# Four sums of weight blocks per chunk, on GpSimd in place of VectorE, in a gated attention and ReGLU kernel

## The chip, the cores and the metric

The kernel runs on one core of a Trainium2 chip. The metric is the device time of one execution in microseconds; the time before is the median of 3 runs. In the profile the engines are called PE (TensorE matmuls), PEld (TensorE weight loads, which overlap PE), DVE (VectorE), ACT (ScalarE), POOL (GpSimd) and SP (SyncE, which issues the DMAs here). L621 is line 621 of the kernel.

## What is computed

Two branches on the same x (2048 tokens, width 576) and a gate between them. Branch a is a linear attention with 32 heads of 18; branch b is a gated feed-forward layer with 4608 hidden columns. All is float32.

```
g = sigmoid(sum(x * gate_w))                      # one gate per token
q, k, v = x @ wqkv, by heads
phi(u) = [softmax(u @ w_phi), softmax(-u @ w_phi)]
a = (phi(q) (phi(k)^T v) / (phi(q) phi(k)^T 1)) @ wo
gate, up = x @ W_gate, x @ W_up                   # 576 x 4608 each
h = max(gate, 0) * up
b = h @ W_down                                    # 4608 x 576
out = g * a + (1 - g) * b
```

The change lies in branch b, in the weights of gate and up.

## The kernel before

**Split operands.** Matmuls run in the format fp32r. To keep float32 accuracy each operand is split: ACT copies it to fp32r (the high part), and DVE subtracts that from the original (the low part). A product is then three matmuls: high by high, high by low, low by high.

**Stages.** The first stage makes queries, keys, values and the attention; its result goes to a DRAM tensor `att`. The second is branch b. It goes through 72 units: two halves of the tokens (1024 each, in two blocks of 512) by 36 chunks of 128 hidden columns (L596). Between the halves the operands made of x are built again (`x_operands`, L560), and the finished tiles of the first half are written out (`finish`, L727).

**Seven products in place of eight.** Gate and up of a chunk, for two blocks of tokens, split along the 576 inputs into two halves of 288, are eight products of blocks. The kernel makes them with seven, of sums and differences of blocks. So a unit needs the four raw blocks of weights and four combinations of them:
- `load_w` (L598) brings the four blocks of a unit into one tile `wr` of 128 partitions by 4 x 384 elements, one of two buffers, by one DMA from SP.
- `split_blocks` (L610) makes `wb`, the split of three raw blocks: an ACT copy (L604) and two DVE subtractions (L607, L608). It serves the products 1, 2 and 4.
- `split_sums` (L617) first overwrites `wr` with the four combinations (L621 to L624, each 128 x 384 elements, each needing the one before), then makes `ws`, the split of all four: the same lines L604, L607, L608. It serves the products 5, 6, 7 and 3.

Both are traced for unit u + 1 while unit u is computed (L795, L801). The tiles `wb` and `ws` have two buffers each.

**One unit on PE.** Each product is seven matmuls at L720, in the order 1, 5, 6, 7, 2, 3, 4. Products 1, 6, 7 and 4 accumulate in one PSUM tile `cx` (two buffers); 5 and 3 in `ca`; 2 in `cy`. Between them the partial results are taken out: ACT copies cx to g1 (L789), ca to u2 (L794), cx to g2 (L800); DVE adds cx to u2 (L805), cy to g1 (L810), ca to g2 (L815). At the end DVE multiplies gate and up (L822), and `split` makes hh and hl of the result (L123, L124).

**The down projection.** `down` (L744) runs for a pair of units, spread as steps between the products of the next pair. Each step is a group of matmuls at L763 into a PSUM tile `pd` (two buffers), which DVE adds to an accumulator in SBUF (L770), or into one of two tiles `pm` that stay in PSUM. `split_down` (L703) prepares its weights `wd`.

**The order of the work.** The program is traced in the order of the code, and a planner then sets the order of each engine's queue from the priorities of the trace and its own costs. On the engine each queue is worked off in that fixed order, an instruction waiting for the semaphores of its inputs and of the buffers it overwrites. Where `in_order` is used (L49: parts of `x_operands` in the first stage's end) the order of the trace is kept on DVE, ACT and SP. POOL serves the first stage only: it scales half of each tile of softmax terms (L182), and sets some constants (L259, L403).

Of the kernel before, what the change touches and what calls it, by code (L numbers as in the profile page):

```python
# [62 lines left out]
def gated_mix_kernel(  # L63
# [25 lines left out]
    nc = tc.nc  # L89
    PSUM = bass.MemoryType.PSUM  # L90
    SUB, ADD, MULT = ALU.subtract, ALU.add, ALU.mult
    tt = nc.vector.tensor_tensor
# [510 lines left out]
    def split_w(o, a, after=None):  # L603
        i = nc.scalar.activation(o[:, :, 0:3], a, AF.Copy)  # L604
        if after:
            tc.add_manual_dep(i.ins, after.ins.name, NO_SYNC, reason="after")
        tt(out=o[:, :, 3:5], in0=a[:, :, 0:2], in1=o[:, :, 0:2].bitcast(F32), op=SUB)  # L607
        tt(out=o[64:96, :, 2], in0=a[64:96, :, 2], in1=o[64:96, :, 2].bitcast(F32), op=SUB)  # L608
# [8 lines left out]
    def split_sums(u):  # L617

        if u < len(units):
            a = RAW.pop(u)  # L620
            tt(out=a[:, 2], in0=a[:, 2], in1=a[:, 3], op=ADD)  # L621
            tt(out=a[:, 3], in0=a[:, 0], in1=a[:, 3], op=SUB)
            tt(out=a[:, 0], in0=a[:, 2], in1=a[:, 0], op=SUB)
            tt(out=a[:, 1], in0=a[:, 1], in1=a[:, 0], op=SUB)  # L624
            o = wop.tile([P, 4, 5, P], F32R, name="ws")
            split_w(o, a)
            WO[u].update({5: (o, 2), 6: (o, 0), 7: (o, 3), 3: (o, 1)})
# [12 lines left out]
    for n, tb in enumerate(order):  # L640
# [23 lines left out]
        if not more:  # L664
            split_blocks(0)
            split_sums(0)
# [115 lines left out]
    for u, (hf, c) in enumerate(units):  # L782
# [16 lines left out]
        g2 = tp.tile([P, TB], F32, name="g2", tag="tp")  # L799
        nc.scalar.activation(g2, cx, AF.Copy)  # L800
        split_sums(u + 1)  # L801
        step()
        product(cx, u, 7, False)
# [117 lines left out]
```

## Time and profile before

| | us |
|---|---|
| median of 3 runs | 1706.8 |
| lowest and highest | 1704.52 and 1708.77 |
| the profiled execution | 1707.41 |
| its span on the core | 1705.6 |

The mean granted clock of PE in the profiled execution is 0.98 of full speed. The groups of instructions which the change touches or which stand next to it, each 72 times in the program (busy us in total, then the mean ns of one):

| line, engine | what | busy us, mean ns |
|---|---|---|
| L622, L623, L624 DVE | sums in wr, 128 x 384 | 40.1, 557 each |
| L604 ACT | copy to ws, 128 x 1536 | 107.3, 1490 |
| L607 DVE | low part of ws, 128 x 1024 | 88.2, 1225 |
| L608 DVE | low part of ws, 32 x 512 | 49.2, 683 |
| L607 DVE | low part of wb, 128 x 768 | 69.0, 958 |
| L608 DVE | low part of wb, 32 x 384 | 39.6, 550 |

A row of the views used below is read so: in the rows of groups, line, engine, operation, output <- inputs, sizes, the count, then busy time and mean, then the idle time of the engine ahead of the group and what ended it. In rows in order of time, the start in us from the beginning of the span and the duration come first; "x7" is seven instructions merged into one row, and the bracket gives the idle time just before and what ended it. In the chain of waits, each piece is on the chain that ended last, followed back from the last instruction.

### The profile page before, as it was taken

How to read it: one execution, taken by the hardware profiler on the slowest of the kernel's cores; microseconds unless marked ns; L12 is line 12 of the kernel's file. 1: busy time of each engine (PE TensorE's matmuls, PEld its weight loads, DVE VectorE, ACT ScalarE, POOL GpSimd, SP SyncE). 2: the span in 40 equal slices, each digit the busy share in tenths (PEclk: the TensorE clock that was granted, in tenths of full speed). 3: DMA queues.
4: the chain of work that ended last, by engine and by line, in shares of the span. 5: the costliest groups of instructions: out<-in, count | busy, mean ns of one | idle time of the engine just before them, and what ended most of it. 6: DMA issues, size and time to landing. Idle time of an engine off the chain costs nothing.

```text
span 1705.6 us, 19899 instructions
## 1 busy us (share of the span) xinstructions
PE 1648.6 (97%) x7834; PEld 1379.0 (81%) x7834; DVE 1291.1 (76%) x1966; ACT 624.0 (37%) x895; POOL 46.0 (3%) x53
## 2 busy tenths in 40 slices
PE   9999997988999999999999998999999999999996
PEld 8899995666888888888888886788888888888885
DVE  5877675666778777777778779977777777777776
ACT  4233335554533333333323334433333332333330
POOL 0121210000000000000000000000000000000000
PEclk9899997889999999999999999999999999999998
DMA  5211113535221211122122212421111222121203
GB/s 182 69 37 58 44 44 96 170 127 169 83 70 65 70 51 60 61 65 70 51 70 66 70 51 70 149 83 62 63 61 52 70 65 70 51 70 60 63 18 105
DMA packets 42329, 128.48 MB, mean 75 GB/s; under 512 B 4906, under 2 KB 5546, under 8 KB 42236
## 3 DMA queue, kind: packets, MB, share of 16 engines
q1 hardware_dynamic: 42236, 127.22, 23.1%
q8 instruction: 61, 1.00, 0.2%
q14 instruction: 32, 0.26, 0.0%
HBM read 108.50 MB, written 16.74 MB: 73 GB/s over the span
## 4 chain that ended last, share of the span: by engine, by line
PE 86%; DVE 5%; DMA 4%; ACT 2%; issue 1%; SPq 1%; DVEq 0%; ACTq 0%
PE cx L720 26%; PE pd L763 19%; PE ca L720 13%; PE cy L720 6%; PE pm L763 5%; PE pq L150 4%; PE pk L150 3%; PE pv L150 3%; PE kv L319 2%; PE pwo L150 2%; PE ptr L283 1%; DMA ga<-att 1%; PE po L150 1%; DMA xr<-xs 1%; DMA wdr<-wd 1%
## 5 line engine op out<-in xcount | busy, mean ns | idle before, releaser
L763 PE MATMUL pd<-hh,wd 128*128 128x512 f32 x1008 | 357.5, 390 | 2.2 <-DVE ac L770 2.2
L720 PE MATMUL cx<-xo,ws 128*128 128x512 f32 x1008 | 253.2, 390 | 5.3 <-DVE ws L608 2.2
L720 PE MATMUL cx<-xo,wb 128*128 128x512 f32 x1008 | 252.5, 390 | 2.8 <-DVE o L556 1.4
L720 PE MATMUL ca<-xo,ws 128*128 128x512 f32 x1008 | 253.4, 390 | 0.8 <-DVE ws L608 0.6
L720 PEld LDWEIGHTS cx<-xo,ws 128*128 128x128 f32 x1008 | 188.8, 188 | 46.6 <-ACT g L789 2.7
L763 PE MATMUL pd<-hl,wd 128*128 128x512 f32 x576 | 224.6, 390 | 0.0
L720 PEld LDWEIGHTS cx<-xo,wb 128*128 128x128 f32 x1008 | 188.9, 188 | 43.8 <-DVE o L556 1.9
L763 PEld LDWEIGHTS pd<-hh,wd 128*128 128x128 f32 x1008 | 189.4, 188 | 43.1 <-DVE ac L770 3.5
L720 PEld LDWEIGHTS ca<-xo,ws 128*128 128x128 f32 x1008 | 189.2, 188 | 42.2 <-ACT wd L708 1.0
L770 DVE TENSOR_TENSOR ac<-pd,ac 128x512 f32<-128x512 f32 x272 | 187.5, 690 | 33.1 <-PE pd L763 33.1
L123 ACT ACTIVATE hh<-g 128x512 fp32r<-128x512 f32 x144 | 83.0, 621 | 294.3 <-DVE g L822 294.3
L708 ACT ACTIVATE wd<-wdr 128x576 fp32r<-128x576 f32 x72 | 48.8, 679 | 262.2 <-PE pd L763 256.0
L604 ACT ACTIVATE ws<-wr 128x1536 fp32r<-128x1536 f32 x72 | 107.3, 1490 | 59.5 <-DVE wr L624 59.5
L720 PE MATMUL cy<-xo,wb 128*128 128x512 f32 x504 | 126.6, 389 | 0.0
L763 PEld LDWEIGHTS pd<-hl,wd 128*128 128x128 f32 x576 | 108.4, 188 | 22.4
L607 DVE TENSOR_TENSOR ws<-wr,ws 128x1024 fp32r<-128x1024 f32 x72 | 88.2, 1225 | 44.1 <-ACT ws L604 43.9
L607 DVE TENSOR_TENSOR wb<-wr,wb 128x768 fp32r<-128x768 f32 x72 | 69.0, 958 | 55.1 <-ACT wb L604 53.5
L720 PEld LDWEIGHTS cy<-xo,wb 128*128 128x128 f32 x504 | 94.6, 188 | 19.6
L763 PE MATMUL pm<-hh,wd 128*128 128x512 f32 x288 | 101.0, 389 | 0.0
L800 ACT ACTIVATE g<-cx 128x512 f32<-128x512 f32 x72 | 43.1, 598 | 153.4 <-PE cx L720 147.4
L822 DVE SCALAR_TENSOR_TENSOR g<-g,cx 128x512 f32<-128x512 f32 x72 | 49.5, 687 | 60.2 <-PE cx L720 60.1
L815 DVE TENSOR_TENSOR g<-ca,g 128x512 f32<-128x512 f32 x72 | 49.8, 691 | 58.4 <-PE ca L720 58.3
(180 smaller groups left out, 2555.2 us busy)
## 6 DMA issues: line engine op xcount, KB each, us to landing
wr<-wgu SPq DMA_DIRECT2D x72, 768.0 KB
wdr<-wd SPq DMA_DIRECT2D x72, 288.0 KB
eT<-et SPq DMA_DIRECT2D x12, 594.0 KB
er<-eT SPq DMA_DIRECT2D x12, 594.0 KB
xr<-xs SPq DMA_DIRECT2D x8, 768.0 KB
att<-o SPq DMA_DIRECT2D x16, 256.0 KB
ga<-att SPq DMA_DIRECT2D x16, 256.0 KB
outT<-o SPq DMA_DIRECT2D x16, 256.0 KB
```

Of the source, the lines that this page charges most:

```text
L123: nc.scalar.activation(hi, src, AF.Copy)
L150: nc.tensor.matmul(ps, w, m, start=i == 0, stop=i == len(pairs) - 1)
L319: nc.tensor.matmul(kv[j // 2][:vn + 1, j % 2, :gn], v[:, j * GS:j * GS + vn + 1], flat(e)[:, c0:c0 + gn], start=False, stop=t == NT - 1, s ...
L604: i = nc.scalar.activation(o[:, :, 0:3], a, AF.Copy)
L607: tt(out=o[:, :, 3:5], in0=a[:, :, 0:2], in1=o[:, :, 0:2].bitcast(F32), op=SUB)
L708: nc.scalar.activation(o[:, :D], w, AF.Copy)
L720: nc.tensor.matmul(ps, w, v, start=first and m == 0, stop=m == len(pairs) - 1, skip_group_check=True)
L763: nc.tensor.matmul(ps, w, v, start=i == 0 and (g == 0 or not perm), stop=i == len(pairs) - 1 and (g == NGR - 1 or not perm))
L770: tt(out=ACC[m, t], in0=ps, in1=ACC[m, t], op=ADD)
L800: nc.scalar.activation(g2, cx, AF.Copy)
L815: tt(out=g2, in0=ca, in1=g2, op=ADD)
L822: nc.vector.scalar_tensor_tensor(out=g, in0=g, scalar=0.0, in1=up, op0=ALU.max, op1=MULT)
```

## The change

The four combinations are issued on GpSimd with the same operands, in the same place of the trace; nothing else is altered.

```diff
         if u < len(units):
             a = RAW.pop(u)
-            tt(out=a[:, 2], in0=a[:, 2], in1=a[:, 3], op=ADD)
-            tt(out=a[:, 3], in0=a[:, 0], in1=a[:, 3], op=SUB)
-            tt(out=a[:, 0], in0=a[:, 2], in1=a[:, 0], op=SUB)
-            tt(out=a[:, 1], in0=a[:, 1], in1=a[:, 0], op=SUB)
+            pt = nc.gpsimd.tensor_tensor
+            pt(out=a[:, 2], in0=a[:, 2], in1=a[:, 3], op=ADD)
+            pt(out=a[:, 3], in0=a[:, 0], in1=a[:, 3], op=SUB)
+            pt(out=a[:, 0], in0=a[:, 2], in1=a[:, 0], op=SUB)
+            pt(out=a[:, 1], in0=a[:, 1], in1=a[:, 0], op=SUB)
             o = wop.tile([P, 4, 5, P], F32R, name="ws")
             split_w(o, a)
             WO[u].update({5: (o, 2), 6: (o, 0), 7: (o, 3), 3: (o, 1)})
```

`tt` is `nc.vector.tensor_tensor`. The subtractions of `split_w` stay on DVE.

## The prediction

> **What bounds the kernel now.** I read the page first: the span and the shares.
>
> ```profile
> span 1705.6 us, 19899 instructions
> ...
> PE 1648.6 (97%) x7834; PEld 1379.0 (81%) x7834; DVE 1291.1 (76%) x1966; ACT 624.0 (37%) x895; POOL 46.0 (3%) x53
> ```
>
> PE is the bound on average and DVE is second. An average says little about a change inside one stage, so I cut the span into stretches (busy us of PE, PEld, DVE, ACT, POOL in each, with counts).
>
> ```profile
> core 0: us, PE busy (x) PEld busy (x) DVE busy (x) ACT busy (x) POOL busy (x), PEclk, DMA share, GB/s
> 380.00:420.00 40.00, 35.68 (x146) 27.83 (x145) 26.96 (x34) 17.36 (x23) 0.00 (x0) 0.96 0.51 166
> 600.00:1018.00 418.00, 418.00 (x1846) 346.24 (x1845) 325.78 (x503) 141.22 (x192) 0.00 (x0) 1.00 0.19 63
> 1018.00:1108.00 90.00, 82.64 (x341) 63.29 (x340) 84.74 (x124) 41.05 (x50) 0.00 (x0) 0.98 0.33 102
> 1036.00:1090.00 54.00, 47.40 (x190) 35.83 (x191) 52.57 (x80) 19.30 (x23) 0.00 (x0) 0.97 0.43 137
> 1108.00:1640.00 532.00, 532.00 (x2348) 440.53 (x2347) 415.05 (x641) 181.93 (x246) 0.00 (x0) 1.00 0.19 63
> ```
>
> There are three places to judge. In the **steady stage** (600 to 1018 and 1108 to 1640) PE is busy for every microsecond, 418.00 of 418.00 and 532.00 of 532.00, so a lighter DVE can gain nothing there; it can only lose. At the **turn** between the two halves (1018 to 1108) PE loses 90.00 - 82.64 = 7.36 us, and within it DVE is busy 52.57 of 54.00 us: here DVE is the bound. At the **start** (380 to 420) PE loses 4.3 us. POOL is empty in all of them.
>
> **What goes.** Four DVE instructions of each of 72 chunks; one of the four groups, with two groups used further down:
>
> ```profile
> L621 DVE TENSOR_TENSOR wr<-wr 128x384 f32<-128x384 f32 x72 | 40.2, 558 | 2.3
> ...
> L604 ACT ACTIVATE wb<-wr 128x1152 fp32r<-128x1152 f32 x72 | 83.3, 1157 | 0.1
> ...
> L259 POOL MEMSET vt<- 128x6 f32 x16 | 1.7, 108 | 40.3 <-ACT gs L258 21.9 <-ACT vt L255 18.4
> ```
>
> That is 4 x 40.2 = 161 us of DVE, and 1291 falls to about 1130.
>
> **What comes.** The same four on POOL. Before, POOL has no sum of 384 elements; its nearest rows are the multiplications of 576 at L182 (minimum/median/maximum ns), and two of them in order of time (start, duration):
>
> ```profile
> L182 POOL TENSOR_TENSOR e<-e,sm x16: 1181/1668/1692, 41.2 to 246.0; 128x576 f32<-128x576 f32 x16
> L182 DVE TENSOR_TENSOR e<-e,sm x16: 758/760/1492, 41.5 to 246.3; 128x576 f32<-128x576 f32 x16
> L182 POOL TENSOR_TENSOR e<-e,r x16: 1163/1168/1176, 67.0 to 264.9; 128x576 f32<-128x576 f32 x16
> ...
> 245.73 0.69 DVE L170 TENSOR_REDUCE mn<-pq 128x32 f32<-128x576 f32 x1
> ...
> 245.98 1.19 POOL L182 TENSOR_TENSOR e<-e,sm 128x576 f32<-128x576 f32 x1 [5.74 <-DVE sm L244]
> 246.34 1.44 DVE L182 TENSOR_TENSOR e<-e,sm 128x576 f32<-128x576 f32 x1
> ```
>
> The queries' product (e<-e,r) takes 1168 ns undisturbed. If all of that scales with the elements, 384 cost 779 ns; if none does, 1168. The memset of 6 elements took 108 ns, so I take 0.11 as the fixed part: 0.11 + (1.17 - 0.11) x 384/576 = 0.82 us. Each sum reads what the one before wrote, so they run one after the other; I allow 0.05 between them and ahead of the first. The chain is 4 x 0.82 + 4 x 0.05 = 3.5 us, with ends at 4 x 0.78 + 0.1 = 3.2 and 4 x 1.17 + 0.2 = 4.9.
>
> The same rows show that the two engines get in each other's way. At 245.98 POOL was first and took 1.19, and DVE's own product, started at 246.34, took 1.44 in place of 0.76. Usually it is POOL that waits: 1668 in place of 1168. The Trainium skill (SBUF — State Buffer, section Who interferes with whom) says that a DVE instruction with two SBUF inputs and a GpSimd instruction that reads SBUF exclude each other for a whole instruction; these rows agree, with 0.5 us lost on POOL or 0.7 on DVE.
>
> **The steady stage.** One chunk there, DVE with the instructions of the others that matter (start, duration):
>
> ```profile
> 813.58 0.56 DVE L621 TENSOR_TENSOR wr<-wr 128x384 f32<-128x384 f32 x1
> ...
> 815.36 0.56 DVE L624 TENSOR_TENSOR wr<-wr 128x384 f32<-128x384 f32 x1
> ...
> 815.95 1.49 ACT L604 ACTIVATE ws<-wr 128x1536 fp32r<-128x1536 f32 x1 [0.54 <-DVE wr L624]
> ...
> 816.18 0.69 DVE L770 TENSOR_TENSOR ac<-pd,ac 128x512 f32<-128x512 f32 x1 [0.26 <-PE pd L763]
> ...
> 817.48 1.23 DVE L607 TENSOR_TENSOR ws<-wr,ws 128x1024 fp32r<-128x1024 f32 x1 [0.61 <-ACT ws L604]
> ...
> 818.72 0.68 DVE L608 TENSOR_TENSOR ws<-wr,ws 32x512 fp32r<-32x512 f32 x1
> ...
> 819.43 0.69 DVE L805 TENSOR_TENSOR u<-cx,u 128x512 f32<-128x512 f32 x1
> ...
> 820.71 0.69 DVE L770 TENSOR_TENSOR ac<-pd,ac 128x512 f32<-128x512 f32 x1
> ...
> 822.30 0.69 DVE L815 TENSOR_TENSOR g<-ca,g 128x512 f32<-128x512 f32 x1 [0.90 <-PE ca L720]
> ...
> 823.46 1.75 PE L720 MATMUL cx<-xo,wb 128*128 128x512 f32 x7
> ...
> 825.04 0.39 PE L763 MATMUL pd<-hh,wd 128*128 128x512 f32 x1
> ...
> 825.70 0.69 ACT L708 ACTIVATE wd<-wdr 128x576 fp32r<-128x576 f32 x1 [8.25 <-PE pd L763]
> ...
> 827.53 0.84 PE L720 MATMUL ca<-xo,ws 128*128 128x512 f32 x3
> ```
>
> The four sums run from 813.58 to 815.92: 2.34 us. On POOL they take 3.5, so the copy to ws, and the DVE instructions behind it, come 1.1 us later (0.9 to 2.6 by the ends). That is the added wait: DVE stands at L607 until POOL and then ACT are done, with L608, L805, L810, L770 and L815 queued behind. Who waits for them:
> - ws is ready at 819.40 and first read at 827.53: cover 8.1 us.
> - L805 is done at 820.12, and PE adds to the same cx at 823.46: cover 3.3 us. This is the shortest.
> - The L770 of 820.71 is done at 821.40 and its bank, one of two, is filled again at 825.04: cover 3.6 us.
> - L815 already waits 0.90 for PE, so a lag of that size ends there.
> - ACT's next instruction behind the copy is L708, after 8.25 idle. POOL has nothing else to do.
> - The next load of wr waits for L608, but a chunk's buffer is read again only later: the 72 copies to wb that read these loads stood idle 0.1 us in all.
>
> So 1.1 us, and even 2.6, lies under 3.3 us: I cost the steady stage at **0**. If the cover went, each microsecond beyond 3.3 would be paid in some 70 chunks. Beside POOL's chain DVE has only L770 to do, which has one input in PSUM; the reduction of a PSUM tile (L170, 245.73) beside the POOL product of 245.98 left that at 1.19, so I expect no clash.
>
> **The turn.** The chain of waits here runs through DVE, sums included, up to the split of ws, and PE waits for that:
>
> ```profile
> 1028.97 0.56 DVE wr L621
> ...
> 1031.20 0.47 DVE wr L622
> ...
> 1035.20 0.56 DVE wr L623
> ...
> 1036.36 0.47 DVE wr L624
> ...
> PE cx L720 <- DVE ws L608: 2.2, 1, 2.2
> ```
>
> The sums' pieces are 0.56 + 0.47 + 0.56 + 0.47 = 2.06 us, about as much as PE's wait for L608 (2.2). They go. What is late next is the rest of DVE's queue, the operands of the second half, and behind them the transfers of the finishing tiles, so I count nothing for the other chunks of the turn. Given back: DVE's work here is mostly SBUF with SBUF, so a POOL sum and a DVE instruction can exclude each other. By the median row POOL waits and DVE loses 0; by the row of 246.34 DVE could lose a whole sum, 0.82. I take 0.15 for each of the four, nearer to the median: 0.6. The turn: -2.06 + 0.6 = **-1.5**, with ends at -7.4 (all that PE loses) and +4 x 0.82 - 2.06 = +1.2 for one chunk.
>
> **The start.**
>
> ```profile
> 380.49 0.56 DVE L621 TENSOR_TENSOR wr<-wr 128x384 f32<-128x384 f32 x1
> ...
> 383.02 0.55 DVE L624 TENSOR_TENSOR wr<-wr 128x384 f32<-128x384 f32 x1
> ...
> 387.34 0.69 DVE L124 TENSOR_TENSOR rdl<-rd,rdh 128x512 fp32r<-128x512 f32 x1 [0.29 <-DMA R<-og]
> ```
>
> Here other work stood between the sums: 380.49 to 383.57, 3.08 us. On POOL 3.5, so 0.4 late, of which 0.29 is hidden by the wait for a DMA at 387.34: **+0.1** (up to 4.9 - 3.08 - 0.29 = +1.5).
>
> **Sum.** 0 - 1.5 + 0.1 = -1.4 us. The profiled execution took 1707.41 us (1705.6 of it span); 1707.4 - 1.4 = 1706.0. Its own lead over the median 1706.8 is 0.6. About 0.3% (5.1 us) is what a measurement of this kernel can tell from no change, and -1.4 lies well inside.
>
> **Rivals.**
> - *DVE's relief empties the turn.* DVE is busy 52.57 of 54.00 us there and loses the sums of three chunks, 3 x 2.2 = 6.7 us. If all of it reaches PE, 1707.4 - 6.7 = 1700.7. For it: the DVE share. Against: transfers end waits in that stretch too, and the sums do not lie in the chain of every chunk. Chance 0.12.
> - *The two engines exclude each other at the turn.* Three chunks with four sums, each holding up DVE by 0.82, cost 9.8 us, less the 2.06 won, plus 1.5 at the start: +9, at 1716. This is the mechanism of the page on SBUF. For it: the row of 1.44. Against: the medians, by which POOL is the one that waits. Chance 0.12.
> - *POOL's chain overruns the cover in the steady stage; slower.* Place: DVE's queue behind L607, ended by PE waiting at the product into cx for L805. Price: if every sum took the 1.67 of the disturbed rows, 4 x 1.67 + 0.2 = 6.9, which is 4.5 late, 1.2 over the cover, in 70 chunks 84 us: 1791. It decides from (2.34 + 3.3 - 0.2) / 4 = 1.36 us a sum. For it: such times occur. Against: only L770 runs beside the sums. Chance 0.06.
> - *The change does not do what it says:* the instructions are named for POOL outright, so only the planned order of the other queues is free. A new order may fill DVE's gap with splits of SBUF data; one or two clashes of 0.5 us still fit under 3.3. It is in the forecast's width.
>
> **How the numbers follow.** Forecast (within 0.3%): 0.70. Faster by over 0.3%: 0.12, the first rival. Slower by over 0.3%: 0.12 + 0.06 = 0.18. The range goes from the first rival's 1700 to just short of the second's 1716: 1700 to 1715; it leaves out the 0.06 and some of the other edges.
>
> **What would show it.** POOL busy at 46 + 288 x 0.82 = 282 us, DVE at about 1130, both long stretches of PE still full, and the copy to ws waiting for POOL about 1.1 us more each. Wrong would be: a sum over 1.36 us in the steady stage; PE waiting for L805 or L770 in every chunk; a turn in which PE loses much more or less than 6 us.

## The result, and the profile after

| | before | after |
|---|---|---|
| median, us | 1705.55 (6 runs, the 3 of the table ahead of the prediction among them) | 1724.82 (6 runs) |
| lowest and highest, us | 1703.57 and 1708.77 | 1718.18 and 1727.52 |
| the profiled execution, us | 1707.41 | 1718.18 |

The ratio after to before (of the means) is 1.0107, with a 95% interval of 1.0087 to 1.0126: some 18 us slower. The profiled execution of after is its fastest; it lies 10.8 us above that of before, and the typical one another 6.6 above it. Part of this is luck ahead of the change: the four matmuls at L504, shortly before the first moved sum (376.2 us), start at 372.3 us in the trace of before and at 367.8 in that of after. Counted from there, the two executions differ by 15.3 us.

The page of after first: its span, the shares of the engines, and three groups (line, engine, operation, tiles, count | busy us, mean ns of one | idle us of the engine just before, and what ended it).

```profile
span 1716.4 us, 19978 instructions
...
PE 1647.0 (96%) x7834; PEld 1376.5 (80%) x7834; DVE 1128.0 (66%) x1678; ACT 622.2 (36%) x895; POOL 344.6 (20%) x341
...
L622 POOL TENSOR_TENSOR wr<-wr 128x384 f32<-128x384 f32 x72 | 74.3, 1032 | 1081.1 <-issue 836.8
...
L607 DVE TENSOR_TENSOR ws<-wr,ws 128x1024 fp32r<-128x1024 f32 x72 | 88.2, 1225 | 196.5 <-ACT ws L604 196.5
L604 ACT ACTIVATE ws<-wr 128x1536 fp32r<-128x1536 f32 x72 | 107.1, 1488 | 211.1 <-POOL wr L625 211.1
```

DVE has lost 1291.1 - 1128.0 = 163 us of work, as it should, and PE has as much work as before, yet the span has grown by 10.8 us. The two big idle times, 196.5 us of DVE at L607 and 211.1 us of ACT at the copy to ws, look like the culprit. Most of that idle time costs nothing, as the same stretches before and after show (us, then busy us and count of PE, PEld, DVE, ACT and POOL, PEclk, DMA share, GB/s). Before:

```profile
420.00:470.00 50.00, 48.12 (x211) 39.11 (x210) 38.33 (x61) 24.44 (x34) 0.00 (x0) 1.00 0.27 86
1015.00:1125.00 110.00, 102.64 (x429) 79.73 (x428) 100.56 (x149) 50.11 (x64) 0.00 (x0) 0.98 0.32 100
```

After:

```profile
380.00:420.00 40.00, 34.17 (x137) 26.67 (x136) 23.98 (x29) 19.00 (x25) 0.80 (x1) 0.91 0.53 175
420.00:470.00 50.00, 46.16 (x198) 36.13 (x197) 28.92 (x41) 20.69 (x30) 16.35 (x16) 1.00 0.23 74
600.00:1018.00 418.00, 418.00 (x1846) 346.16 (x1845) 266.37 (x408) 142.03 (x192) 97.30 (x96) 1.00 0.19 62
1015.00:1125.00 110.00, 95.19 (x390) 73.69 (x389) 91.13 (x120) 43.53 (x54) 25.08 (x20) 0.97 0.31 97
1125.00:1660.00 535.00, 535.00 (x2362) 443.04 (x2362) 342.37 (x523) 183.68 (x250) 124.14 (x123) 1.00 0.19 61
```

The steady stage is full of PE as before: 418.00 of 418.00, 535.00 of 535.00, with the same 1846 and 2362 matmuls. PE's idle time grew at the turn, from 7.36 to 14.81 us (+7.45), and at the start, from 4.32 to 5.83 in 380 to 420 (+1.5) and from 1.88 to 3.84 in 420 to 470 (+2.0). That makes 10.9 us of idle time. It equals the difference of the spans by chance: it leaves out the 4.5 us by which after was ahead at L504, and what PE loses while it is busy at a reduced clock (PEclk 0.91 against 0.96 in 380 to 420).

So the stages are timed by PE's own work as well, from the L504 group to the first matmul into `cy` (product 2) of units 6, 34, 42 and 71, counted from 0. The start, up to unit 6, takes 148.6 us before and 154.8 after (+6.2). From unit 6 to 34 it is 488.69 in both, and from 42 to 71 it is 506.15 in both. The turn, from unit 34 to 42, takes 152.7 before and 161.6 after (+8.9).

What PE waits for at the turn, 1015 to 1125, by the view of the waits of after (us in all, times, longest), and DVE's wait there for ACT's copy, which was 0.4 us before:

```profile
PE cx L721 <- DVE u L806: 6.0, 2, 3.2
PE pd L764 <- DVE ac L771: 3.2, 3, 1.4
PE ca L721 <- DVE ws L608: 2.7, 1, 2.7
...
DVE ws L607 <- ACT ws L604: 8.6, 4, 2.4
```

PE waits for DVE still, although DVE has less to do. The rows of the first unit of the turn in order of time, DVE and POOL of after, show why:

```profile
1028.24 1.01 POOL L622 TENSOR_TENSOR wr<-wr 128x384 f32<-128x384 f32 x1 [16.48 <-ACT xo L569]
...
1028.74 1.59 DVE L570 TENSOR_TENSOR xo<-xr,xo 128x1024 fp32r<-128x1024 f32 x1
1029.33 1.88 POOL L623 TENSOR_TENSOR wr<-wr 128x384 f32<-128x384 f32 x1
1030.35 1.40 DVE L571 TENSOR_TENSOR xo<-xr,xo 32x512 fp32r<-32x512 f32 x1
1031.28 1.34 POOL L624 TENSOR_TENSOR wr<-wr 128x384 f32<-128x384 f32 x1
1031.78 2.46 DVE L583 TENSOR_TENSOR xr<-xr,xr 128x1536 f32<-128x1536 f32 x1
1032.71 2.41 POOL L625 TENSOR_TENSOR wr<-wr 128x384 f32<-128x384 f32 x1
1034.16 2.57 DVE L580 TENSOR_TENSOR xr<-xr,xr 128x1536 f32<-128x1536 f32 x1
...
1039.83 1.22 DVE L570 TENSOR_TENSOR xo<-xr,xo 128x1024 fp32r<-128x1024 f32 x1
1041.06 0.68 DVE L571 TENSOR_TENSOR xo<-xr,xo 32x512 fp32r<-32x512 f32 x1
```

L570 and L571 take 1.22 and 0.68 us when POOL is idle (last two rows), L583 and L580 1.75 (in pool_writes; L580 is shown below). Beside POOL they take 1.59, 1.40, 2.46 and 2.57: DVE loses 0.37 + 0.72 + 0.71 + 0.82 = 2.62 us for four POOL sums, more than the 2.06 us that the prediction credits for the sums. POOL loses too: its four sums last from 1028.24 to 1035.12, 6.9 us. The ends show that the two take turns: L623 ends at 1031.21, and L571, which starts at 1030.35, ends 0.54 behind that; L624 ends at 1032.62, 0.87 behind the end of L571; and so on down the rows.

In the steady stage the same four sums meet nothing of that kind (DVE, POOL and ACT of after, in order of time):

```profile
815.39 1.01 POOL L622 TENSOR_TENSOR wr<-wr 128x384 f32<-128x384 f32 x1 [13.08 <-issue]
...
817.89 0.69 DVE L771 TENSOR_TENSOR ac<-pd,ac 128x512 f32<-128x512 f32 x1 [2.63 <-PE pd L764]
818.67 1.01 POOL L625 TENSOR_TENSOR wr<-wr 128x384 f32<-128x384 f32 x1
819.71 1.49 ACT L604 ACTIVATE ws<-wr 128x1536 fp32r<-128x1536 f32 x1 [2.59 <-POOL wr L625]
821.23 1.23 DVE L607 TENSOR_TENSOR ws<-wr,ws 128x1024 fp32r<-128x1024 f32 x1 [2.66 <-ACT ws L604]
```

The chain takes 819.68 - 815.39 = 4.29 us, and the one DVE instruction beside it, L771 with one operand in PSUM, takes its 0.69.

### The profile page after: what moved, and what is told of

It reads as the page before. It is cut to its first block, busy times and chain, and to the rows that moved or that the text cites. A ratio compares the mean times of both kernels' runs of the same rounds, so it can differ in the third digit from the quotient of the medians.

```text
span 1716.4 us, 19978 instructions
## 1 busy us (share of the span) xinstructions
PE 1647.0 (96%) x7834; PEld 1376.5 (80%) x7834; DVE 1128.0 (66%) x1678; ACT 622.2 (36%) x895; POOL 344.6 (20%) x341
## 5 line engine op out<-in xcount | busy, mean ns | idle before, releaser
L771 DVE TENSOR_TENSOR ac<-pd,ac 128x512 f32<-128x512 f32 x272 | 186.6, 687 | 175.3 <-PE pd L764 175.2
L622 POOL TENSOR_TENSOR wr<-wr 128x384 f32<-128x384 f32 x72 | 74.3, 1032 | 1081.1 <-issue 836.8
L607 DVE TENSOR_TENSOR ws<-wr,ws 128x1024 fp32r<-128x1024 f32 x72 | 88.2, 1225 | 196.5 <-ACT ws L604 196.5
L604 ACT ACTIVATE ws<-wr 128x1536 fp32r<-128x1536 f32 x72 | 107.1, 1488 | 211.1 <-POOL wr L625 211.1
L607 DVE TENSOR_TENSOR wb<-wr,wb 128x768 fp32r<-128x768 f32 x72 | 69.0, 958 | 52.0 <-ACT wb L604 50.3
L124 DVE TENSOR_TENSOR hl<-g,hh 128x512 fp32r<-128x512 f32 x144 | 93.0, 687 | 2.4 <-ACT hh L123 2.1
```

The lines of the kernel that those rows point to most:

```text
L124: tt(out=lo, in0=src, in1=hi.bitcast(F32), op=SUB)
L622: pt(out=a[:, 2], in0=a[:, 2], in1=a[:, 3], op=ADD)
L771: tt(out=ACC[m, t], in0=ps, in1=ACC[m, t], op=ADD)
```

## The experiments

Two theories stood from the start. **Exclusion** (A and A1 in the expectations): where POOL's sums lie beside DVE's instructions with two SBUF operands (turn and start), each holds the other up. **Wait and order**: ws comes later, since ACT's copy now waits for POOL, so that DVE's queue stands at L607 (A2), and the planner has written all queues anew (C). B is a small loss in every chunk. The times below are medians; the ratio is to the kernel before on the same chip, with its 95% interval.

### Where it is lost: after_again, steady, turn, entry

```diff
-            pt = nc.gpsimd.tensor_tensor
+            pt = nc.gpsimd.tensor_tensor if (5 <= u < NC or u >= NC + 4) else tt    # steady
+            pt = nc.gpsimd.tensor_tensor if NC <= u < NC + 4 else tt                # turn
+            pt = nc.gpsimd.tensor_tensor if u < 5 else tt                           # entry
```

`after_again` is the changed kernel as it is. Of the other three, each has POOL sums in one stage alone and DVE sums elsewhere. PE, ACT and SP of `steady` have the order of before. By the traces, PE's queue has that order in `entry` too, and in `turn` that of the changed kernel.

> The changed kernel once more, for a second trace and more times; the profiled execution of it took 1718 us and its other runs 1723 to 1728. Theory A (POOL sums at the entry and at the turn lose PE time, partly through the half clock that follows a gap of PE): 1718 to 1728, with PE again full from 600 to 1018, PE losing 11 to 14 us at the turn and 3 to 5 us between 420 and 460. Rival B (a small loss in every chunk of the steady stage that the first trace happened not to show): the second trace shows PE gaps spread over 600 to 1018 and 1108 to 1640 of 5 us or more in all.

> Sums on POOL only in units 5 to 35 and 40 to 71, on DVE at the entry and around the turn; PE, ACT and SP keep the order of the kernel before. Theory A: as the kernel before, 1703 to 1709, ratio 0.998 to 1.002, with POOL sums near 1.01 us each and PE full in the steady stage. Rival B (loss in every chunk): 63 of 72 chunks keep the sums on POOL, so most of the 19 us stays: 1718 to 1724.

> Sums on POOL only in units 36 to 39, around the turn between the halves. Theory A: the larger part of the loss, 6 to 13 us over the kernel before, that is 1712 to 1719, with DVE instructions stretched beside POOL sums and PE waiting for L806 and L771 at the turn. Rival B: 4 of 72 chunks, about +1 us: 1705 to 1708.

> Sums on POOL only in units 0 to 4, at the entry into the second stage. Theory A: the smaller part, +2 to +8 us, 1708 to 1714. Rival B: 5 of 72 chunks, about +1 us: 1705 to 1708.

| | us | ratio | PE idle 420 to 470, 1015 to 1125 | start, turn by PE's work |
|---|---|---|---|---|
| before | | | 1.88, 7.36 | 148.6, 152.7 |
| after_again | 1724.83 (4 runs) | 1.0098 [1.0081, 1.0115] | 3.73, 14.67 | 154.5, 161.4 |
| steady | 1707.66 (12) | 1.0007 [0.9990, 1.0023] | 1.12, 10.47 | 147.9, 156.2 |
| turn | 1715.38 (6) | 1.0049 [1.0032, 1.0066] | 0.46, 13.84 | 148.0, 161.9 |
| entry | 1713.30 (5) | 1.0035 [1.0021, 1.0049] | 4.11, 7.85 | 156.0, 151.7 |

The 63 units of the steady stage cost nothing that can be measured; the trace of `steady` loses 3.5 us at the turn, where the sums of units 40 and 41 are on POOL already, while its 12 runs allow 0.23% (3.9 us) at most. The four units of the turn cost 0.49%, the planner's new order there included, and the five of the start 0.35%. The three together (0.91%) come near to the whole (0.98 to 1.07%). In the start the clash is the same, only with other instructions. Two rows of DVE and two of POOL, of after:

```profile
424.01 1.01 POOL L624 TENSOR_TENSOR wr<-wr 128x384 f32<-128x384 f32 x1
...
424.12 1.45 DVE L710 TENSOR_TENSOR wd<-wdr,wd 128x512 fp32r<-128x512 f32 x1 [1.21 <-ACT wd L709]
...
425.10 1.32 POOL L625 TENSOR_TENSOR wr<-wr 128x384 f32<-128x384 f32 x1
...
433.12 0.69 DVE L710 TENSOR_TENSOR wd<-wdr,wd 128x512 fp32r<-128x512 f32 x1
```

The split of the down weights, 0.69 us by itself, takes 1.45 beside POOL, behind the sum that began at 424.01.

### What POOL does to DVE: pool_reads, pool_writes

Both are the kernel before, sums on DVE, with idle work for POOL in units 0 to 4 and 36 to 39. Nobody waits for that work, and every queue but POOL's has the order of before, so wait and order are out of it.

```diff
             tt(out=a[:, 1], in0=a[:, 1], in1=a[:, 0], op=SUB)
+            if u < 5 or NC <= u < NC + 4:
+                wb = WO[u][1][0].bitcast(F32)
+                for _ in range(4):                                # pool_reads
+                    nc.gpsimd.tensor_tensor(out=idle, in0=wb[:, 0, 2:5], in1=wb[:, 1, 2:5], op=ADD)
+                nc.gpsimd.tensor_tensor(out=idle[:, :, 0:1], in0=wb[:, 0, 2:5, 0:1], in1=wb[:, 1, 2:5, 0:1], op=ADD)
+                for _ in range(10):                               # pool_writes (this and the line above)
+                    nc.gpsimd.memset(idle, 0.0)
```

> The kernel before, with the sums on DVE and every queue in its order; in units 0 to 4 and 36 to 39 POOL also makes four additions of 384 elements from wb into a spare tile, behind the split of wb, for which nobody waits. A1: DVE's instructions beside them are stretched by up to 0.8 us at each POOL addition, as in the changed kernel (L583 2.46 in place of 1.75); at the turn and the entry, where DVE is behind, this reaches PE: +3 to +10 us, 1710 to 1717. A2 and C: no wait is added and no order changed: 1704 to 1709.

> As the run with the additions, but POOL makes one tiny addition and then ten memsets of 384 elements in the same place, some 4 us that only write. A1, if it is the reading that excludes: DVE's instructions keep their lengths, 1704 to 1709. If any POOL work beside DVE costs: as with the additions, 1710 to 1717. A2 and C: 1704 to 1709.

pool_reads: 1719.09 us (4 runs), 1.0077 [1.0060, 1.0093], 2 us above the range expected of A1. pool_writes: 1707.57 us (12), 1.0003 [0.9990, 1.0016]. The first unit of the turn in pool_reads:

```profile
1029.04 5.67 POOL L629 TENSOR_TENSOR idle<-wb 128x384 f32<-128x384 f32 x4 [556.74 <-ACT xo L569]
...
1029.51 1.63 DVE L570 TENSOR_TENSOR xo<-xr,xo 128x1024 fp32r<-128x1024 f32 x1
1031.15 1.40 DVE L571 TENSOR_TENSOR xo<-xr,xo 32x512 fp32r<-32x512 f32 x1
...
1033.77 2.56 DVE L580 TENSOR_TENSOR xr<-xr,xr 128x1536 f32<-128x1536 f32 x1
```

And in pool_writes:

```profile
1027.07 4.72 POOL L630 MEMSET idle<- 128x384 f32 x10
...
1027.27 1.22 DVE L570 TENSOR_TENSOR xo<-xr,xo 128x1024 fp32r<-128x1024 f32 x1
1028.51 0.68 DVE L571 TENSOR_TENSOR xo<-xr,xo 32x512 fp32r<-32x512 f32 x1
...
1029.69 1.75 DVE L580 TENSOR_TENSOR xr<-xr,xr 128x1536 f32<-128x1536 f32 x1
```

The additions stretch DVE's instructions just as the sums of the changed kernel do, though no result of theirs is used; POOL's writes, 4.72 us of them, stretch nothing. So the clash is with POOL's reads. The Trainium skill (SBUF — State Buffer, section Who interferes with whom) says so: a DVE instruction with two SBUF inputs contends with a GpSimd instruction that reads SBUF, not with one that only writes. The rows agree on both sides (1.63 against 1.22; 1.22 beside the writes), and with L771's 0.69 in the steady stage. In pool_reads DVE's own sums, which have two SBUF operands too, are caught as well (L622 took 1.26 there), so its 0.77% is no measure of what the changed kernel loses to the clash.

### What the order does: pool_old_order, dve_new_order, reads_new_order

```diff
+    traced = nc.cur_bb.bb.instructions
+    for row in json.loads(zlib.decompress(base64.b85decode(QUEUES))):
+        at, prev = 0, None
+        for gap in row:
+            at += gap
+            i = traced[at]
+            if prev is not None:
+                tc.add_manual_dep(i, prev.name, NO_SYNC, reason="replay")
+            prev = i
```

`QUEUES` holds a recorded order of a queue; the planner then keeps to it, and no wait is added. pool_old_order is the changed kernel in the order of before (DVE: without the sums). dve_new_order is the kernel before in the order of the changed one, with DVE's sums behind the split of wb. reads_new_order is pool_reads in that order.

> All sums on POOL, with the queues of PE, ACT and SP held to the order that they have in the kernel before, and DVE's to the same order without the sums. Theory A1 (POOL's reads and DVE's instructions with two SBUF inputs exclude each other) and A2 (the longer chain of sums makes DVE stand at L607, with L771 and L806 behind it): the loss stays, 1716 to 1732, since neither needs a new order. Rival C (the planner's new order of PE, ACT and DVE at the entry and the turn is what costs): 1704 to 1709.

> All sums on DVE, each four of them right behind the split of wb, with the queues of PE, ACT, SP and the rest of DVE in the order of the changed kernel. A1 and A2: no POOL sums, no loss of that kind; 1704 to 1711, the order being made for other costs. Rival C: the loss stays, 1717 to 1728.

> Sums on DVE in the order of the changed kernel, with POOL's four additions for which nobody waits in units 0 to 4 and 36 to 39. A1: the exclusion costs as in the old order, +10 to +16 us, 1716 to 1723. If the exclusion only costs in the old order: 1705 to 1711.

pool_old_order: 1712.51 us (5 runs), 1.0037 [1.0023, 1.0052], between the two expectations. dve_new_order: 1708.44 (11), 1.0013 [0.9999, 1.0027], in the range of A1 and A2 and not of C. reads_new_order: 1730.95 (5), 1.0147 [1.0124, 1.0169], 8 us above the higher expectation; it has DVE's sums and POOL's additions, so more to clash than the changed kernel. The changed kernel loses 1.07% in its own order and 0.37% in that of before, so the planner's order matters; but with the sums on DVE that order costs little. Neither theory has the whole by itself. What is left is whether the wait for POOL, without its reads, costs something.

### The wait without the reads: late_old_order, late_new_order, held_new_order, writes_for_sums, writes_old_order

The first two are the kernel before in the two orders, with POOL writes that were to hold ACT's copy to ws.

```diff
+                nc.gpsimd.tensor_tensor(out=idle[:, :, 0:1], in0=wb[:, 0, 2:5, 0:1], in1=wb[:, 1, 2:5, 0:1], op=ADD)
+                for _ in range(8):
+                    nc.gpsimd.memset(idle, 0.0)
+                nc.gpsimd.memset(o[:, 0, 0, 0:1].bitcast(F32), 0.0)
```

> The kernel before with every queue in its order and the sums on DVE; in units 0 to 4 and 36 to 39 POOL runs nine memsets (some 4.3 us, writes only) behind the split of wb, and the last of them writes one column of ws, so that ACT's copy to ws can't start before: the wait of the changed kernel without its reads. The additions that nobody waits for cost 13 us, POOL sums in this order 6.4. A1 (the exclusion makes all of the loss): 1703 to 1710. A2 (standing at L607 with L770 and L805 behind makes part of it): +3 to +8 us, 1709 to 1715.

> The same wait in the order of the changed kernel, sums on DVE right behind the split of wb. That order with sums on DVE and no wait took 1708 us. A1: 1705 to 1712. A2 in the new order (the planner put L607 ahead of L770 and L805 there, so that DVE stands in front of them): +6 to +14 us over the kernel before, 1712 to 1721.

1707.47 us (12 runs), 1.0006 [0.9994, 1.0018], and 1709.74 (12), 1.0021 [1.0006, 1.0036]. Both are inconclusive: the copy was not held. Nothing tied the last write to the others, so it did not stand behind them for its own unit. ACT and POOL of late_new_order at the turn:

```profile
1026.12 3.76 POOL L631 MEMSET idle<- 128x384 f32 x8
...
1027.87 1.50 ACT L604 ACTIVATE ws<-wr 128x1536 fp32r<-128x1536 f32 x1 [2.37 <-DVE wr L625]
...
1030.77 0.10 POOL L632 MEMSET ws<- 128x1 f32 x1 [0.90 <-PE ca L728]
```

The copy starts at 1027.87, released by DVE's sum, while POOL's writes run on to 1029.88. The edit below ties the writes together, and two more runs follow it: the changed kernel with nine POOL writes in place of the four sums, in its own order and in that of before. These two leave the four sums out, so ws is made of constants.

```diff
+                for i, prev in zip(chain[1:], chain):                        # held_new_order
+                    tc.add_manual_dep(i.ins, prev.ins.name, NO_SYNC, reason="chain")
...
-            pt(out=a[:, 2], in0=a[:, 2], in1=a[:, 3], op=ADD)
-            pt(out=a[:, 3], in0=a[:, 0], in1=a[:, 3], op=SUB)
-            pt(out=a[:, 0], in0=a[:, 2], in1=a[:, 0], op=SUB)
-            pt(out=a[:, 1], in0=a[:, 1], in1=a[:, 0], op=SUB)
+            prev = None                                                      # writes_*
+            for k in (2, 2, 2, 3, 3, 0, 0, 1, 1):
+                i = nc.gpsimd.memset(a[:, k], 0.01)
+                if prev is not None:
+                    tc.add_manual_dep(i.ins, prev.ins.name, NO_SYNC, reason="chain")
+                prev = i
```

> The sums are VectorE's, in the order of the changed kernel on all queues; in units 0 to 4 and 36 to 39 ScalarE's copy to ws is held by a chain of POOL writes, kept in order, that begins behind the split of wb and takes about 4.3 us. VectorE so does its sums and has the late ws as well. Theory A1: 1705 to 1712 us (1708.4 for this order without the hold, and little more). Theory A2 (the late ws is what costs): 1713 to 1721 us, with VectorE standing at L607 for 1.5 to 2.5 us in the units of the turn.

> The changed kernel in its own order on every queue, but the four sums of each unit are replaced by nine chained POOL writes of a constant of 384 elements (about 4.2 us by the 0.47 us each of pool_writes, beside the 4.28 us of the sums); it leaves the four sums out, so ws is made of constants. ScalarE's copy and VectorE's split at L607 wait behind POOL as in the changed kernel, but POOL reads nothing. Theory A1 (the loss is POOL's reads and VectorE's two-input instructions shutting each other out): 1700 to 1709 us, VectorE's L570, L571, L580 and L583 back at about 1.22, 0.68, 1.75 and 1.75 us, and PE's loss in 1015 to 1125 at most 8 us. Theory A2 (the loss is the longer way to ws, which leaves VectorE standing at L607): 1712 to 1722 us, with the loss in 1015 to 1125 above 11 us.

> The kernel of writes_for_sums (the four sums of each unit replaced by nine chained POOL writes of a constant, so the sums are left out and ws is made of constants) with TensorE's, ScalarE's and SyncE's queues and the rest of VectorE's held to the order of the kernel before: the fourth field of a table whose other three are pool_old_order (reads, old order, 1712.5 us), the changed kernel (reads, new order, 1724.8) and writes_for_sums (no reads, new order, 1711.9). The wait of ScalarE's copy for POOL is there, the reads are not. If what writes_for_sums had left (+6 us) comes of the planner's order, this run gives 1703 to 1708 us, and the reads alone cost 5 to 9 us in the old order. If it comes of the wait for POOL in any order, it gives 1710 to 1714 us, and the reads cost nothing in the old order.

held_new_order: 1717.33 us (6 runs), 1.0067 [1.0048, 1.0086]; in the new order the wait costs time with next to no read of POOL, one of 3 elements in each chain (1.0013 without the hold). DVE has the sums to do as well there, which it has not in the changed kernel, so the figure is an upper one. writes_for_sums: 1711.94 (11), 1.0036 [1.0023, 1.0049], between the two expectations: most of the loss goes with the reads, a third stays. writes_old_order: 1704.30 (11), 1.0004 [0.9995, 1.0013]: nothing stays. The four fields together, with PE's idle time in 1015 to 1125 and DVE's wait at L607 for ws there, in us of the profiled executions:

| | order of before | the planner's own order |
|---|---|---|
| POOL writes, no reads | 1.0004; 7.65, 4.4 | 1.0036; 8.81, 6.0 |
| POOL sums | 1.0037; 10.69, 3.3 | 1.0107; 14.81, 8.6 |

The row of the turn in writes_old_order, in the columns of the stretches above, is that of a kernel without a clash (7.36 was lost before):

```profile
1015.00:1125.00 110.00, 102.35 (x436) 80.29 (x435) 90.54 (x127) 49.32 (x63) 21.59 (x54) 1.00 0.33 103
```

Read down, POOL's reads cost 0.33% (5.6 us) in the old order and 0.71% (12 us) in the new. Read across, the new order costs 0.32% (5.5 us) without the reads and 0.70% with them. By the ratios the two do more than add: together they cost 18 us, against 5.6 + 5.5 + 0.7 = 12 us one by one. But that excess, 0.38%, has an interval of some 0.3% either way (an estimate from the intervals of the four ratios), and the traces do not show it. Start and turn by PE's work take 301.3 us before; with the writes 299.9 in the old order and 308.9 in the new, with the sums 309.1 in the old and 316.4 in the new. From 299.9, reads cost 9.2 and the order 9.0, and both 16.5. So it is not shown that each makes the other dearer. The same figures show where the new order costs, with the wait for POOL in it: with the writes, the turn takes 151.1 us in the old order and 156.8 in the new, the start 148.8 and 152.1, while PE's idle time at the turn differs by 1.2 us only. The writes take 3.88 us in place of 4.28, which makes their wait a little shorter than the real one. That ws holds constants does not change PE's pace: unit 6 to 34 takes 488.69 us in these traces too.

So: exclusion makes nearly all of the loss in the old order and two thirds of it in the planner's; a longer wait alone does nothing that can be measured as long as the queues keep their old order, and in the planner's order the same lateness reaches PE. DVE stands longest at L607 where both come together (8.6 us). Which of the reordered instructions at the turn does it was not told apart.

## Why the prediction was wrong, step by step

**What bounds the kernel.** Right: PE in the steady stage, DVE at the turn. It is this that made a slower path through DVE at the turn cost time.

**What goes and comes.** DVE fell to 1128.0 us (about 1130 predicted). A POOL sum was mis-sized, 0.82 us where it takes 1.01. All four groups, of which the first and the last are quoted, have a median of 1.01 to 1.02 (minimum/median/maximum ns):

```profile
L622 POOL TENSOR_TENSOR wr<-wr x72: 1005/1013/1467, 376.2 to 1657.8; 128x384 f32<-128x384 f32 x72
...
L625 POOL TENSOR_TENSOR wr<-wr x72: 1008/1011/2412, 379.8 to 1661.0; 128x384 f32<-128x384 f32 x72
```

The second and third sum do not read what the one before wrote, as the prediction has it, they overwrite what it reads; on one queue the four run one after the other all the same. The fixed part of a POOL instruction was taken from a memset, 0.11 us. From 384 and 576 elements (1.01 and 1.17 us) the line through both has some 0.7 us at no elements; the two come from different stages of the kernel, so that is an estimate. The chain came to 4.29 us instead of 3.5, inside its ends of 3.2 and 4.9, and POOL was busy 344.6 us instead of 282.

**The steady stage at 0.** Right, and for the reason given: the chain is 4.29 - 2.34 = 1.95 us later than DVE's sums were, under the cover of 3.3. PE lost no microsecond there (488.69 us from unit 6 to 34 in the trace of every run), and `steady` gave 1.0007. The rival by which the cover is overrun fell with it.

**The turn, the step that failed.** It was put at -1.5 us and came to +8.9 by PE's work, the planner's new order included. Two of its terms were wrong.
- *Given back, 0.15 us for each sum, 0.6 in all.* It was 0.65 each in the first unit, 2.62 in all, in place of 0.6. The row picked for the size, the median of the first stage's products, was one of POOL waiting while DVE lost nothing. There one POOL product met one DVE product; at the turn a chain of four sums met a row of four DVE instructions, and with each hand-over the other engine waited once. The row of 246.34 (DVE 0.7 late), which was quoted and set aside as the rarer case, was the right one.
- *The sums' 2.06 us go.* They left DVE, but not the path to ws: ACT's copy waits for POOL in their place, and DVE at L607 for the copy, 4.4 us at the turn in writes_old_order against 0.4 before. That run has the relief, and no clash, and gains nothing: 1.0004, -1 to +2 us. The first rival, by which the relief empties the turn, fell with it.

**The start at +0.1.** Wrong in the same way: 0.35% by `entry`, about 6 us, and +6.2 by PE's work in the trace of after. Only the chunk at 380 was looked at, and only for lateness; the clash with the splits of wd behind 420 was left out, although these have two SBUF operands as well.

**A new order in the forecast's width.** Wrong. It was priced at one or two clashes of 0.5 us under the cover of the steady stage. The order did its harm at turn (5.7 us) and start (3.3 us, both between the two kernels with POOL's writes), where there is no such cover.

**The rival that came true.** That the two engines exclude each other at the turn was the mechanism, at a chance of 0.12. Its price of 9 us lies between what the reads cost by the ratios in the old order (5.6 us) and in the new (12), but it knew nothing of the order's share; the time came out 9 us above its 1716 and outside the range, whose upper end had been put just under it.

No version here beat the kernel before by what can be measured: writes_old_order, which has all of the relief and none of the clash, is at 1.0004.

## What to carry to other kernels

An operation moved from DVE to POOL is priced at the place where it will run: list what DVE does beside it, and for every DVE instruction there with two SBUF operands charge DVE some two thirds of a POOL instruction (0.65 of 1.01 us on average in the first unit of the turn) for each hand-over, and let POOL's chain grow by as much. A result that left an engine's queue is still on the path if the next reader waits for it. And when a planner writes the queues anew, price its new order too: here, holding the old order took away two thirds of the loss.

## What was not expected of the hardware

**Turn-taking holds through a whole chain.** Neither engine keeps the access to itself: four sums and four DVE instructions alternated one by one, and both rows grew, DVE's by 2.62 us and POOL's from 4.29 to 6.9.

**A gap on PE goes on costing when it is over.** PE in after, behind its longest wait at the turn:

```profile
1039.37 3.25 PE L721 MATMUL cx<-xo,wb 128*128 128x512 f32 x8 [3.25 <-DVE u L806]
1042.42 0.63 PE L764 MATMUL pm<-hh,wd 128*128 128x512 f32 x1
...
1043.82 1.75 PE L721 MATMUL cx<-xo,ws 128*128 128x512 f32 x7
```

Behind 3.25 us of idle time eight matmuls take 3.25 us, 0.41 each; a little later seven take 1.75, 0.25 each. The granted clock is 0.51 of full speed from 1040.0 to 1043.3 us and 1.00 from 1043.5 to 1046.0. Idle time of PE by the view of the stretches does not hold this loss; the time between two matmuls of known units does.

Of the 6.6 us that the typical runs of after have over the profiled one, a part lies ahead of the change. The second trace (after_again, 1721.17 us) is 3.0 us above the first, but its start and turn took no longer (154.5 and 161.4 us against 154.8 and 161.6): its L504 group starts at 371.3 us, 3.6 later. Over the traces of all runs that group starts between 366.1 and 373.4 us. The runs of 1723 us and more had a mean granted clock of 0.975 to 0.978, against 0.982 in the profiled one of after; none of them left a trace, so where they lose the rest stays open.
